# Retention attention followed by a gated feed-forward block on one core: products of 64x64 on quarters of TensorE for pairs 2 to 11

## The chip, the cores and the metric

The kernel runs on one core of a Trainium2 chip. The metric is the device time of one execution in microseconds (us). TensorE (PE in the profile, with its weight loads as PEld) multiplies matrices into PSUM; VectorE (DVE), ScalarE (ACT) and GpSimd (POOL) do the elementwise work; SyncE (SP) issues transfers. Each engine takes its instructions in the order in which the kernel lists them.

## The reference, cut to what matters

Two stages follow each other, on 4 batch entries, 8 heads, 768 tokens and head size 64; the feed-forward block has model width 512 and inner width 1536.

```python
gamma = 1.0 - 2.0 ** (-5.0 - arange(H))
for t in range(S):
    state = gamma * state + einsum('bhd,bhe->bhde', k[:, :, t], v[:, :, t])
    y[:, :, t] = D ** -0.5 * einsum('bhd,bhde->bhe', q[:, :, t], state)
x = y.transpose(0, 2, 1, 3).reshape(B * S, H * D)
out = (sigmoid(x @ w_gate) * (x @ w_val)) @ w_out
```

## The kernel before, in words

**Tiles and pairs.** The 768 tokens are 6 token tiles of 128. A tile holds 4 batch entries; the kernel takes them two at a time, so there are 12 pairs P (tile P // 2, entries 2(P % 2) and the next, called c = 0 and 1). The recurrence is done in chunks: within a tile by scores, across tiles by a running state.

**The steps of a pair.** Each step is a short function that emits instructions; a two-letter name and a number call it from a list.

- `lk`, `lq`, `lv`: GpSimd loads k, q, v of a pair (L64), tokens on partitions. A tile of 1024 columns holds 16 heads of 64.
- `xk`, `xq` (pairs 4 to 11): SyncE issues one transposing transfer of the whole tile (L197) into `qkT`, so that head dimensions lie on partitions. Two heads share a block of 128 partitions: head 2p in the lower half, 2p+1 in the upper. For pairs 2 and 3 TensorE transposes (`tp`, L178) and ScalarE copies (`te`, L188).
- `sc`: scores of one entry, eight products with 64 rows of contraction and 128 columns of output (L216), two running side by side on the upper and lower half of the array, into two PSUM banks. `sd` is both entries.
- `mk`: VectorE multiplies four heads of scores with the decay mask (L221); four of these for a pair. The number is 4P + 2c + i.
- `in`: the inter products, query with the state of earlier tiles (L233). The state of two heads lies block-diagonally in `zbd`, with zeros beside it, so each product contracts over 128 rows and gives 64 columns; two run side by side on the left and right half. `id` is both entries.
- `ia`: the intra products, masked scores with v (L239), added on the same bank. `il` is both entries. `yo`: VectorE scales the result into `xT`, the input of the feed-forward block (L254). The number of `in`, `ia`, `yo` and `sc` is 2P + c.
- `kt`, `sm`, `zs`, `zo`: keys are scaled (L206, L209), k times v is formed (L261), added to the state on VectorE (L270), and copied to `zbd` by ScalarE in two halves (L274, two steps).
- `ho`: a tiny copy on GpSimd (L556) that reads the last transposed element of a pair, so that later loads are issued only after that.

**The feed-forward block** is done for one token tile at a time (512 rows). From tile 3 on, and for the down projection from tile 0 on, it uses products of halves with sums and differences prepared beforehand, so it has many small steps: `gm`, `vm`, `ag`, `av`, `bg`, `bv`, `vp` (up products, L284 whole or L288 split), `sg`, `as`, `bs` (sigmoids on ScalarE), `mu`, `am`, `bm` (gating on VectorE), `vc`, `va`, `vf` (copy, add and finish), `dm`, `dp`, `dc`, `da`, `ds` (down products, copy, add and store), and the sums `hs`, `hh` (VectorE, L460), `xs` (VectorE), `aw`, `dw`, `wp` (GpSimd, L339 and L443).

**Whole and split products.** A step in small letters emits its products in column halves: 128 rows by 64 columns, two side by side (L288). In capitals it emits 128 by 128 (L284). So the array is used in three shapes: 128x128, 128 rows x 64 columns, and 64 rows x 128 columns (only the scores).

**What sets the order.** Nothing is scheduled automatically. `ORDER` is one string for each token tile; its steps are emitted in that order, `+` and `-` shift a step to a later or an earlier tile. The place of a step fixes the place of its instructions in the queue of every engine that it uses. PSUM gives seven banks to everything but the state products, which have an eighth to themselves.

Of the kernel before, what the change touches and what calls it, by code (L numbers as in the profile page):

```python
# [17 lines left out]
def kernel(  # L18
# [40 lines left out]

    def load(P, *what):  # L60
        for n in what:
            held, x = {"k": (kn, k), "q": (qn, q), "v": (vn, v)}[n]
            held[P] = ld.tile([C, 2 * H, D], BF16, tag=n, name=n + "n", bufs=4)
            nc.gpsimd.dma_start(out=held[P], in_=src(x, P))  # L64

    def load_one(P, c, *what):
        for n in what:
            held, x = {"k": (kn, k), "q": (qn, q), "v": (vn, v)}[n]
            if P not in held:
                held[P] = ld.tile([C, 2 * H, D], BF16, tag=n, name=n + "n", bufs=4)  # L70
            t, j = divmod(P, 2)
            nc.gpsimd.dma_start(out=heads(held[P], c),
                                in_=x[2 * j + c, :, t * C:(t + 1) * C, :].rearrange("h s d -> s h d"))
# [56 lines left out]
    zbd = [const.tile([128, 2, NP, C], BF16, name=f"zbd{i}") for i in range(2)]  # L130
    for z in zbd:
        nc.vector.memset(z, 0.0)
# [33 lines left out]
    def new_qkT(P):  # L166
        qkT[P] = ld.tile([128, 2, 2, NP, C], BF16, tag="qkT", name="qkT", bufs=4)
# [3 lines left out]
    def transpose(P, i, cs):  # L171
        tp = bank([128, 2 * NP, C], BF16).rearrange("d (c p) s -> d c p s", c=2)
        x = (kn, qn)[i][P].rearrange("s g d -> s (g d)")
        for c in cs:
            for p in range(NP):
                for lo, n in ((0, C),) if whole[0] else ((0, D), (D, D)):
                    at_p = (c * NP + p) * C + lo
                    nc.tensor.transpose(tp[lo:lo + n, c, p, :], x[:, at_p:at_p + n], ident)  # L178
        turned[P, i] = tp

    def turned_out(P, i, cs, *evict):
# [5 lines left out]
        for c, e in zip(cs, evict):  # L187
            (nc.scalar.copy if e == "a" else nc.vector.tensor_copy)(qkT[P][:, i, c], tp[:, c])  # L188
# [5 lines left out]
    def xbar(P, i):  # L194
        if P not in qkT:
            new_qkT(P)
        nc.sync.dma_start_transpose(out=qkT[P][:, i].rearrange("d c p s -> d (c p) s"),  # L197
                                    in_=(kn, qn)[i][P].rearrange("s g d -> s (g d)"))
# [12 lines left out]
    def scores(P, c):  # L211
        sc[P, c] = (bank([128, NP, C]), bank([128, NP, C]))
        for p in range(NP):
            for i in range(2):
                half = slice(i * D, (i + 1) * D)
                nc.tensor.matmul(sc[P, c][i][:, p, :], qkT[P][half, 0, c, p, :], qkT[P][half, 1, c, p, :],  # L216
                                 start=True, stop=True)

    def mask(P, c, i):
        st[P, c, i] = at.tile([128, NP, C], BF16, tag="st", name="st", bufs=8)  # L220
# [6 lines left out]
    def inter(P, c):  # L227
        y[P, c] = bank([128, NP, C])
        if P > 1:
            for p in range(NP):  # L230
                for i in range(2):
                    half = slice(i * D, (i + 1) * D)
                    nc.tensor.matmul(y[P, c][half, p, :], zbd[P % 2][:, c, p, half], qkT[P][:, 1, c, p, :],  # L233
                                     start=(p == 0), stop=False, skip_group_check=True)

    def intra(P, c):
        for p in range(NP):
            for i in range(2):
                nc.tensor.matmul(y[P, c][i * D:(i + 1) * D, p, :], heads(vn[P], c)[:, 2 * p + i, :],  # L239
                                 st[P, c, i][:, p, :], start=(P < 2 and p == 0), stop=True, skip_group_check=True)  # L240
# [15 lines left out]
    def state(P):  # L256
        zz[P] = pz.tile([128, 2, NP, D], F32, tag="z", name="z")
        for c in range(2):
            for p in range(NP):
                for i in range(2):  # L260
                    nc.tensor.matmul(zz[P][i * D:(i + 1) * D, c, p, :], heads(kt[P], c)[:, 2 * p + i, :],  # L261
# [10 lines left out]
    def state_out(P, i):  # L272
        half = slice(i * D, (i + 1) * D)
        nc.scalar.copy(zbd[P % 2][half, :, :, half], za[P % 2][half])  # L274
# [78 lines left out]
    def late_weight_sums(g, i):  # L353
        if g not in gws:
            tag = "qqqqkkk"[g]
            room = ld.tile([C, 2 * H, D], BF16, tag=tag, name=tag + "n", bufs=4)
# [198 lines left out]
    def hold(P):  # L555
        nc.gpsimd.tensor_copy(kept[:, :2], qkT[P][:, :, 1, NP - 1, C - 1])  # L556
# [5 lines left out]
    def y_step(P, c, eng="a"):  # L562
        inter(P, c)
# [49 lines left out]
    for s in range(4):  # L613
# [52 lines left out]
        "in": lambda t, n: inter(n // 2, n % 2),  # L666
        "sd": lambda t, P: [scores(P, c) for c in range(2)],
        "id": lambda t, P: [inter(P, c) for c in range(2)],
# [6 lines left out]
        "zo": lambda t, n: state_out(n // 2, n % 2),  # L675
# [92 lines left out]
```

## Time and profile before

| what | value |
|---|---|
| median of 3 runs | 221.34 us (220.79 to 224.9) |
| the profiled execution's own time | 221.63 us |
| its span, first to last instruction | 219.9 us |
| first product starts, last product ends | 2.0 us, 216.4 us |
| PE busy from 18 to 43 us of the span | 24.78 of 25 us |
| PE busy from 43 to 66 us | 23.00 of 23 us |
| PE busy from 66 to 220 us | 150.43 of 154 us |
| DVE, ACT, POOL busy | 158.4, 116.3, 131.1 us |
| granted TensorE clock | 1.000 |

The span is taken by the hardware profiler; 1.7 us of the execution's own time lie around it. Groups of instructions are listed by source line, engine, operation and tiles; behind the bar stand the busy time of the group, the mean duration of one instruction, and the idle time of the engine before them. Matmuls overlap, so the mean of one (some 220 ns for 128 columns) is its latency, not what it adds: that is seen in the timeline, where the start of the next group follows. The chain of work that ended last goes back from the end of the program, at each step to what released it.

### The profile page before, as it was taken

To read this page: it belongs to the slowest core of one execution; us is meant where nothing else is said; L and a number is where in the kernel's file an instruction comes from. 1 tells how busy PE (TensorE), PEld (TensorE's weight loads), DVE (VectorE), ACT (ScalarE), POOL (GpSimd) and SP (SyncE) were. 2 spreads that over 40 slices of the span, in tenths; PEclk is the share of its full clock that TensorE was granted. 3 is DMA by queue.
4 is the path that set the end of the run, shared out by engine and by line. 5 is a ranking of instruction groups with operands and counts; after the bars stand their busy time and mean duration, and the time that the engine had idled before them with its cause. 6 is when DMAs were issued, how large, how long until landed. Compare 5 with 4: busy or idle time off the path is not lost.

```text
span 219.9 us, 6868 instructions
## 1 busy us (share of the span) xinstructions
PE 210.8 (96%) x2906; PEld 163.2 (74%) x2906; DVE 158.4 (72%) x330; ACT 116.3 (53%) x254; POOL 131.1 (60%) x149
## 2 busy tenths in 40 slices
PE   6778999999999999999999999999999999999993
PEld 6565455799888767777778877789877866887782
DVE  6574865988649799766898677699775776555771
ACT  7474366437856165743729554525356626354431
POOL 8978785779997993597037733660281660166700
PEclk9999999999999999999999999999999999999999
DMA  9999999999995999599993999800520000022005
GB/s 127 136 171 195 193 174 160 194 190 157 144 113 93 157 156 167 131 173 166 123 185 46 162 211 149 92 0 3 146 98 0 3 1 3 0 95 97 3 1 192
DMA packets 103999, 25.35 MB, mean 115 GB/s; under 512 B 93984, under 2 KB 101152, under 8 KB 103968
## 3 DMA queue, kind: packets, MB, share of 16 engines
q0 software_dynamic: 81248, 13.90, 84.1%
q1 hardware_dynamic: 22576, 10.88, 27.8%
q8 instruction: 22, 0.36, 0.7%
q10 hardware_dynamic: 144, 0.13, 0.2%
q14 instruction: 9, 0.07, 0.1%
HBM read 28.31 MB, written 6.29 MB: 157 GB/s over the span
## 4 chain that ended last, share of the span: by engine, by line
PE 94%; DVE 3%; ACT 1%; issue 1%; DVEq 0%
PE ff L288 53%; PE ff L284 28%; PE ff L216 3%; PE ff L178 2%; PE ff L239 2%; PE ff L531 2%; PE ff L233 2%; PE z L261 1%; DVE st L221 1%; DVE qkT L188 1%; ACT xT L252 0%; DVE qn L572 0%; DVE xT L252 0%; DVE lgp L117 0%; ACT ob L504 0%
## 5 line engine op out<-in xcount | busy, mean ns | idle before, releaser
L308 ACT ACTIVATE gs<-ff 128x512 f32<-128x512 f32 (+1 forms) x61 | 35.7, 591 | 35.1 <-PE ff L288 23.0
L288 PE MATMUL ff<-xT,wg 128*64 128x512 bf16 (+1 forms) x408 | 48.4, 363 | 0.0
L405 POOL TENSOR_TENSOR hT<-gs,scr 128x512 bf16<-128x512 f32 x17 | 21.9, 1291 | 40.0 <-DVE scr L399 35.9
L288 PE MATMUL ff<-xT,wv 128*64 128x256 bf16 (+1 forms) x352 | 35.7, 324 | 0.0
L288 PEld LDWEIGHTS <-wg 128*64 128x64 bf16 x408 | 23.0, 110 | 10.3 <-issue 0.2
L399 DVE TENSOR_TENSOR scr<-scr,ff 128x256 f32<-128x256 f32 x51 | 20.4, 415 | 13.1 <-PE ff L284 6.0
L288 PEld LDWEIGHTS <-wv 128*64 128x64 bf16 x388 | 21.9, 110 | 8.6
L221 DVE TENSOR_TENSOR st<-ff,maskd 128x512 bf16<-128x512 f32 x40 | 25.7, 683 | 3.5 <-PE ff L216 3.4
L284 PE MATMUL ff<-xT,wg 128*128 128x256 bf16 (+1 forms) x136 | 25.2, 323 | 1.5 <-ACT xT L252 0.9
L311 DVE TENSOR_TENSOR hT<-gs,ff 128x512 bf16<-128x512 f32 (+1 forms) x27 | 17.7, 664 | 7.9 <-PE ff L284 3.0
L288 PEld LDWEIGHTS <-hT 128*64 128x64 bf16 x372 | 20.5, 110 | 3.2
L514 DVE TENSOR_TENSOR ob<-p,ff 128x256 f32<-128x256 f32 x33 | 13.6, 416 | 10.0 <-ACT p L506 4.5
L284 PEld LDWEIGHTS <-wg 128*128 128x128 bf16 x136 | 13.1, 98 | 8.3 <-issue 0.9
L408 POOL TENSOR_TENSOR hT<-gs,scr 128x256 bf16<-128x256 f32 x17 | 12.6, 747 | 6.6 <-DVE scr L399 6.1
L209 ACT ACTIVATE kt<-kn,tabk 128x128 bf16<-128x128 bf16 x48 | 16.4, 393 | 0.0
L254 DVE TENSOR_TENSOR xT<-ff,taby 128x512 bf16<-128x512 f32 x20 | 13.5, 685 | 3.4 <-PE ff L239 3.4
L288 PE MATMUL ff<-wo,hT 128*64 128x256 bf16 (+1 forms) x204 | 15.7, 292 | 0.0
L284 PE MATMUL ff<-xT,wv 128*128 128x256 bf16 (+1 forms) x96 | 15.5, 290 | 0.0
L64 POOL DMA_DIRECT2D vn<-in_v_dram x12 | 14.0, 1170 | 2.3 <-DMA wo<-in_moe_w_out_dram 0.8
L64 POOL DMA_DIRECT2D kn<-in_k_dram x11 | 12.9, 1175 | 3.3 <-DMA vn<-in_v_dram 1.7
L288 PEld LDWEIGHTS <-hs 128*64 128x64 bf16 x252 | 13.7, 110 | 0.4
L274 ACT CAST zbd<-za 64x512 bf16<-64x512 f32 x20 | 12.2, 613 | 3.3 <-DVE za L268 3.1
(108 smaller groups left out, 411.9 us busy)
## 6 DMA issues: line engine op xcount, KB each, us to landing
out_dram<-ob SPq DMA_DIRECT2D x22, 256.0 KB, 2.6
vn<-in_v_dram POOLq DMA_DIRECT2D x12, 256.0 KB, 11.1
kn<-in_k_dram POOLq DMA_DIRECT2D x11, 256.0 KB, 10.3
qn<-in_q_dram POOLq DMA_DIRECT2D x11, 256.0 KB, 11.8
wo<-in_moe_w_out_dram POOLq DMA_DIRECT2D x4, 384.0 KB, 13.0
wg<-in_moe_w_gate_dram POOLq DMA_DIRECT2D x5, 256.0 KB, 9.2
wv<-in_moe_w_val_dram POOLq DMA_DIRECT2D x5, 256.0 KB, 9.3
out_dram<-ob SPq DMA_DIRECT2D x3, 128.0 KB, 2.2
```

The source lines that it names most:

```text
L64: nc.gpsimd.dma_start(out=held[P], in_=src(x, P))
L209: nc.scalar.activation(to[:, :, h, :], x[:, :, h, :], AX.Copy, scale=tabk[:, P // 2, h:h + 1])
L221: nc.vector.tensor_tensor(st[P, c, i], sc[P, c][i], (mask0 if P < 2 else maskd[P // 2])[:, i], op=ALU.mult)
L254: nc.vector.tensor_tensor(o, y[P, c], taby[t], op=ALU.mult)
L284: nc.tensor.matmul(o, left, right, skip_group_check=True, **kw)
L288: nc.tensor.matmul(o[half], left[:, half], right, skip_group_check=True, **kw)
L308: nc.scalar.activation(gated[t, n1][:, lo:hi], us[t, n1, 0][:, lo:hi], AX.Sigmoid)
L311: nc.vector.tensor_tensor(hidden(t)[:, n1, lo:hi], gated[t, n1][:, lo:hi], us[t, n1, 1][:, lo:hi], op=ALU.mult)
L399: nc.vector.tensor_tensor(o, o, (b if n == 5 else ac)[:, :256], op=ALU.add)
L405: nc.gpsimd.tensor_tensor(h[:, 2 * g], s, vals[t, g][:, 0:2].rearrange("p two n -> p (two n)"), op=ALU.mult)
L408: nc.gpsimd.tensor_tensor(h[:, 2 * g + 1, 256:], s[:, 256:], vals[t, g][:, 2], op=ALU.mult)
L514: nc.vector.tensor_tensor(o, x, z, op=ALU.add)
```

## The change

It does five things.

1. For pairs 2 to 11 a score product is cut into two halves of its output rows, 64 rows by 64 columns each (four quarters of the array are used in turn): 16 products in place of 8 for each entry, the same columns streamed.
2. The inter products contract over the 64 rows of their own head only, on one quarter of the array: 16 products of 64 by 64 for a pair, as many as before. Both entries are emitted as one step `id`. The heads of the second entry (c = 1) lie exchanged: what was in the lower half of the partitions lies in the upper, so its products read the other quarters. `zb` holds the state without zeros.
3. The state goes to `zb` in one ScalarE copy of 128 partitions (`zo`, one step) in place of two of 64. The two memsets of `zbd` at the start are gone.
4. To get the exchanged layout, the transposing transfer is issued as two: the first entry's four blocks, and five blocks that begin one head earlier for the second. k and q tiles are 64 columns wider, and GpSimd clears these columns with a memset before it issues the load (pairs 4 to 11). TensorE's transposes for pairs 2 and 3 place each head by itself; their number stays. The tiles `st` have 7 buffers in place of 8.
5. `ORDER` is new from the first tile's last third on, for all engines.

The intra step of a pair names the last four inter products as what it depends on; in the built program no product waits for a semaphore on that account.

```diff
+    def natural(n, P):
+        if n == "v":
+            return ld.tile([C, 2 * H, D], BF16, tag=n, name=n + "n", bufs=4)
+        wide[n, P] = ld.tile([C, 2 * H + 1, D], BF16, tag=n, name=n + "n", bufs=4)
+        if P > 3:
+            nc.gpsimd.memset(wide[n, P][:, 2 * H], 0.0)
+        return wide[n, P][:, :2 * H]
...
-    zbd = [const.tile([128, 2, NP, C], BF16, name=f"zbd{i}") for i in range(2)]
-    for z in zbd:
-        nc.vector.memset(z, 0.0)
+    zb = [const.tile([128, 2, NP, D], BF16, name=f"zb{i}") for i in range(2)]
...
+    def place(P, c, h):
+        return h % 2 ^ (c if P > 1 else 0), c * NP + (h + (c if P > 3 else 0)) // 2
+
+    def of(P, i, c, h):
+        r, b = place(P, c, h)
+        return qkT[P][r * D:(r + 1) * D, i, b, :]
...
-        nc.sync.dma_start_transpose(out=qkT[P][:, i].rearrange("d c p s -> d (c p) s"),
-                                    in_=(kn, qn)[i][P].rearrange("s g d -> s (g d)"))
+        x = wide["kq"[i], P].rearrange("s g d -> s (g d)")
+        nc.sync.dma_start_transpose(out=qkT[P][:, i, :NP], in_=x[:, :H * D])
+        nc.sync.dma_start_transpose(out=qkT[P][:, i, NP:], in_=x[:, (H - 1) * D:])
...
-                half = slice(i * D, (i + 1) * D)
-                nc.tensor.matmul(sc[P, c][i][:, p, :], qkT[P][half, 0, c, p, :], qkT[P][half, 1, c, p, :],
-                                 start=True, stop=True)
+                h = 2 * p + i
+                for u in range(1 if P < 2 else 2):
+                    own = slice(0, C) if P < 2 else slice(u * D, (u + 1) * D)
+                    nc.tensor.matmul(sc[P, c][i][own, p, :], of(P, 0, c, h)[:, own], of(P, 1, c, h),
+                                     start=True, stop=True)
...
-        st[P, c, i] = at.tile([128, NP, C], BF16, tag="st", name="st", bufs=8)
+        st[P, c, i] = at.tile([128, NP, C], BF16, tag="st", name="st", bufs=7)
...
-                    nc.tensor.matmul(y[P, c][half, p, :], zbd[P % 2][:, c, p, half], qkT[P][:, 1, c, p, :],
-                                     start=(p == 0), stop=False, skip_group_check=True)
+                    r, _ = place(P, c, 2 * p + i)
+                    m = nc.tensor.matmul(y[P, c][i * D:(i + 1) * D, p, :], zb[P % 2][r * D:(r + 1) * D, c, p, :],
+                                         of(P, 1, c, 2 * p + i), start=(p == 0), stop=False, skip_group_check=True)
...
-    def state_out(P, i):
-        half = slice(i * D, (i + 1) * D)
-        nc.scalar.copy(zbd[P % 2][half, :, :, half], za[P % 2][half])
+    def state_out(P):
+        nc.scalar.copy(zb[P % 2], za[P % 2])
...
     ORDER = [
...
-        "gm9 vm9 sg9 mu9 tp4 te4 tp5 te5 gm10 vm10 sg10 mu10 sc4 sc5 sm2 mk8 mk9 mk10 mk11 gm11 vm11 sg11 in4+  "
-        "in5+ ia4+ ia5+ yo4+ yo5+ mu11 zs2+ kt24+ tp6+ te6+ tp7+ te7+",
+        "sg9 mu9 tp4 te4 tp5 te5 gm10 vm10 sc4 mk8 sc5 gm11 sg10 mk10 mk9 mk11 tp6+ id2+ ia4+ sg11 ia5+ yo4+  "
+        "tp7+ vm11 yo5+ te6+",
...
-        "wc4 ho5 mk17 dm6- am10 lk6 kt37 mk21 wc5 mk22 hh9- in11 hh11- kt39 mk20 lq6 aw16+ mk23 kt40 dc05- yo9  "
-        "in8 ia8 kt44 ia11 in10 dm7- yo8 ia10 lv6 yo11 lk7 lq7 da05- dp03- dp06- dc06- do3- dt3- lv7 bm10 yo10  "
-        "dp02 hh10- kt43 kt42 kt53+ tt10 sm4",
+        "sc10 aw12+ mk22 kt37 hh11- da05- lq6 dp03- wc5 kt38 id4 id5 kt40 kt45 mk21 kt46 ia8 kt41 mk23 ia9 kt39  "
+        "dp06- ia11 mk20 lv6 aw2+ dm6- kt47 lk7 ia10 kt34 bv10 dm7- dt1- kt44 kt53+ yo11 sm4 hs4 hh6- yo8 yo10  "
+        "lq7 aw14+ wp11 dp01 hh10- aw8+ yo9 aw16+",
-        "gm3 vm1 gm1 gm2 da06-- ds06-- hs0- kt45- zs4- dp07-- hs1- aw12 xk6- aw8 sg1 vm0 vm5 aw1 sm5- da07--  "
+        "gm3 dc06-- lv7- do3-- vm1 hs0- bm10- kt42- gm2 sg2 aw1 da06-- hs8- dt3-- zs4- hs9- dp07-- ds06-- gm0  "
...
```

More of the change, by code (lines that the diff above doesn't have):

```diff
@@ L58, in src @@
         return x[2 * j:2 * j + 2, :, t * C:(t + 1) * C, :].rearrange("b h s d -> s (b h) d")
+    wide = {}
+    def natural(n, P):
[5 more added lines that the diff above has]
+        return wide[n, P][:, :2 * H]
     def load(P, *what):
@@ L62, in load @@
             held, x = {"k": (kn, k), "q": (qn, q), "v": (vn, v)}[n]
-            held[P] = ld.tile([C, 2 * H, D], BF16, tag=n, name=n + "n", bufs=4)
+            held[P] = natural(n, P)
             nc.gpsimd.dma_start(out=held[P], in_=src(x, P))
@@ L69, in load_one @@
             if P not in held:
-                held[P] = ld.tile([C, 2 * H, D], BF16, tag=n, name=n + "n", bufs=4)
+                held[P] = natural(n, P)
             t, j = divmod(P, 2)
@@ L166, in new_qkT @@
     def new_qkT(P):
-        qkT[P] = ld.tile([128, 2, 2, NP, C], BF16, tag="qkT", name="qkT", bufs=4)
+        qkT[P] = ld.tile([128, 2, 2 * NP + 1, C], BF16, tag="qkT", name="qkT", bufs=4)
+    def place(P, c, h):
[3 more added lines that the diff above has]
+        return qkT[P][r * D:(r + 1) * D, i, b, :]
     whole, turned = [True], {}
@@ L175, in transpose @@
             for p in range(NP):
-                for lo, n in ((0, C),) if whole[0] else ((0, D), (D, D)):
-                    at_p = (c * NP + p) * C + lo
-                    nc.tensor.transpose(tp[lo:lo + n, c, p, :], x[:, at_p:at_p + n], ident)
+                if P < 2:
+                    nc.tensor.transpose(tp[:, c, p, :], x[:, (c * NP + p) * C:(c * NP + p + 1) * C], ident)
+                    continue
+                for r in range(2):
+                    g = 2 * (c * NP + p) + (r ^ c)
+                    nc.tensor.transpose(tp[r * D:(r + 1) * D, c, p, :], x[:, g * D:(g + 1) * D], ident)
         turned[P, i] = tp
@@ L187, in turned_out @@
         for c, e in zip(cs, evict):
-            (nc.scalar.copy if e == "a" else nc.vector.tensor_copy)(qkT[P][:, i, c], tp[:, c])
+            (nc.scalar.copy if e == "a" else nc.vector.tensor_copy)(
+                qkT[P][:, i, :2 * NP].rearrange("d (c p) s -> d c p s", c=2)[:, c], tp[:, c])
     def transposes(P, i, cs, *evict):
@@ L225, in masks, with inter @@
             mask(P, c, i)
[L227 to L230, printed above, removed]
-                for i in range(2):
-                    half = slice(i * D, (i + 1) * D)
-                    nc.tensor.matmul(y[P, c][half, p, :], zbd[P % 2][:, c, p, half], qkT[P][:, 1, c, p, :],
-                                     start=(p == 0), stop=False, skip_group_check=True)
+    begun = {}
+    def inter(P):
+        y[P, 0], y[P, 1] = bank([128, NP, C]), bank([128, NP, C])
+        begun[P] = []
+        for p in range(NP):
+            for c in range(2):
+                for i in range(2):
+                    r, _ = place(P, c, 2 * p + i)
+                    m = nc.tensor.matmul(y[P, c][i * D:(i + 1) * D, p, :], zb[P % 2][r * D:(r + 1) * D, c, p, :],
+                                         of(P, 1, c, 2 * p + i), start=(p == 0), stop=False, skip_group_check=True)
+                    if p == NP - 1:
+                        begun[P].append(m.ins)
     def intra(P, c):
@@ L238, in intra @@
             for i in range(2):
-                nc.tensor.matmul(y[P, c][i * D:(i + 1) * D, p, :], heads(vn[P], c)[:, 2 * p + i, :],
-                                 st[P, c, i][:, p, :], start=(P < 2 and p == 0), stop=True, skip_group_check=True)
+                m = nc.tensor.matmul(y[P, c][i * D:(i + 1) * D, p, :], heads(vn[P], c)[:, 2 * p + i, :],
+                                     st[P, c, i][:, p, :], start=(P < 2 and p == 0), stop=True,
+                                     skip_group_check=True)
+                if begun.get(P):
+                    for b in begun.pop(P):
+                        tc.add_manual_dep(m.ins, b.name, mybir.DependencyInfo(
+                            mybir.DependencyClass.Sync, mybir.DependencyReason.DATA), reason="other rows")
     def y_out(P, c, eng="a"):
@@ L260, in state @@
                 for i in range(2):
-                    nc.tensor.matmul(zz[P][i * D:(i + 1) * D, c, p, :], heads(kt[P], c)[:, 2 * p + i, :],
+                    r = i ^ c
+                    nc.tensor.matmul(zz[P][r * D:(r + 1) * D, c, p, :], heads(kt[P], c)[:, 2 * p + i, :],
                                      heads(vn[P], c)[:, 2 * p + i, :], start=True, stop=True, skip_group_check=True)
@@ L270, in state_sum @@
             nc.vector.tensor_tensor(za[j], za[j], zz[P], op=ALU.add)
-    def state_out(P, i):
-        half = slice(i * D, (i + 1) * D)
-        nc.scalar.copy(zbd[P % 2][half, :, :, half], za[P % 2][half])
+    def state_out(P):
+        nc.scalar.copy(zb[P % 2], za[P % 2])
     hT = {}
@@ L355, in late_weight_sums @@
             tag = "qqqqkkk"[g]
-            room = ld.tile([C, 2 * H, D], BF16, tag=tag, name=tag + "n", bufs=4)
+            room = ld.tile([C, 2 * H + 1, D], BF16, tag=tag, name=tag + "n", bufs=4)[:, :2 * H]
             gws[g] = room.rearrange("p (i kk a) d -> p i kk (a d)", i=4, kk=KT // 2)
@@ L555, in hold @@
     def hold(P):
-        nc.gpsimd.tensor_copy(kept[:, :2], qkT[P][:, :, 1, NP - 1, C - 1])
+        nc.gpsimd.tensor_copy(kept[:, :2], qkT[P][:, :, 2 * NP, C - 1])
     def hold_for_sums(t):
@@ L562, in y_step @@
     def y_step(P, c, eng="a"):
-        inter(P, c)
+        y[P, c] = bank([128, NP, C])
         intra(P, c)
@@ L665 @@
         "sc": lambda t, n: scores(n // 2, n % 2),
-        "in": lambda t, n: inter(n // 2, n % 2),
         "sd": lambda t, P: [scores(P, c) for c in range(2)],
-        "id": lambda t, P: [inter(P, c) for c in range(2)],
+        "id": lambda t, P: inter(P),
         "il": lambda t, P: [intra(P, c) for c in range(2)],
@@ L674 @@
         "zs": lambda t, P: state_sum(P),
-        "zo": lambda t, n: state_out(n // 2, n % 2),
+        "zo": lambda t, P: state_out(P),
     }
```

92 rows, old and new, of the table ORDER are left out of this document.

## The prediction

> **What bounds the kernel now.** I read the page's busy times first, then the windows by stage, then the chain in order of time, then the groups with their shapes kept apart, and at last the timelines of SP, DVE and POOL around the places that the new order touches.
>
> ```profile
> span 219.9 us, 6868 instructions
> ...
> PE 210.8 (96%) x2906; PEld 163.2 (74%) x2906; DVE 158.4 (72%) x330; ACT 116.3 (53%) x254; POOL 131.1 (60%) x149
> ...
> PE 94%; DVE 3%; ACT 1%; issue 1%; DVEq 0%
> ```
>
> The first two lines are the page's head and part 1, the third opens part 4. TensorE is busy for 96% and is 94% of the chain. The table above says where the rest is: 0.2 us idle between 18 and 43 us, none from 43 us to the last product at 216.4 us. So until something else runs late, the time is the length of TensorE's stream, and relief for another engine gives nothing.
>
> ```profile
> 46.52 0.55 PE ff L216 x16
> ...
> 50.94 0.45 PE ff L233 x16
> 51.38 0.45 PE ff L239 x16
> ```
>
> These are pieces of the chain: start, length, what. Sixteen products of 128 columns take 0.45 us (inter, intra), because two run side by side: eight rounds of 56 ns. In the trace the second of a round starts 3 to 4 ns after the first, the next round 52 or 53 ns after that. The sixteen score products are eight such rounds too, and take 0.55. The 0.10 above is the change from 64x128 back to 128x64. Single starts show both ways: 205 ns from the last 256-column round to the first score product where the next round would start after 106, and 145 ns from the last score product where 52 is usual. I take 96 ns for a change of shape, the mean of the 99 and the 93.
>
> ```profile
> L216 PE MATMUL ff<-qkT 64*128 64x128 bf16 x192 | 8.7, 225 | 0.6 <-DVE qkT L188 0.5
> ...
> L233 PE MATMUL ff<-qkT,zbd 128*64 128x128 bf16 x160 | 7.1, 219 | 0.0
> ...
> L274 ACT CAST zbd<-za 64x512 bf16<-64x512 f32 x20 | 12.2, 613 | 3.3 <-DVE za L268 3.1
> ```
>
> The groups by shape give the counts and the state copy's price.
>
> **The change part by part.** The profiled execution took 221.63 us, 0.29 above the median of 221.34. I sum against it and take the sum to the median at the end.
>
> *Inter products.* Ten pairs, 0.45 us each now. Afterwards the 16 products are four rounds of four. No row shows four at once. A round is at least the 56 ns of a round of two, and at most that plus two more starts of 3.5 ns, 63. I take 60, since starts cost 3 to 4 ns wherever they are seen: 0.24 a pair, 0.21 saved, **-2.1** in all (-2.0 to -2.25).
>
> *Scores.* Twenty entries, now four rounds of 56 = 0.224. Afterwards 16 products in four rounds of four, 0.24 by the same choice: **+0.3** (0 to +0.56).
>
> *Changes of shape.* Counted in the two built programs, TensorE's stream changes shape 38 times before and 55 after, because `id` steps now stand alone between 128x64 work. 17 at 96 ns: **+1.6**. Forty of the 55 are between 64x64 and 128x64, where only the rows change, and no row shows that kind. The lower bound is nothing for these 40: 15 x 0.096 against 38 x 0.096, -2.2. I take 96 ns, because both kinds that are seen, one that changes rows and columns and one that changes columns alone (128x128 to 128x64, 202 where 109 is usual), cost the same. The page TensorEngine Tiling (Array Packing) of the Trainium skill, Key Properties, says that changing the tiling mode, not just the tile, drains TensorE; the 0.10 of L216 agrees, and by that rule the +1.6 stands, which speaks against this change.
>
> *State copy and memsets.* ScalarE loses ten copies of 0.61 us, DVE two memsets of 0.49 at 3 to 4 us. ScalarE is off the path at 53%, and DVE's next work there waits for a load that lands at 3.9 us: **0**.
>
> *Transposing transfers.* Sixteen issues become 32, with nine blocks moved where there were eight, all on SP's queue; stores behind them (`ds`, `dt`) wait for two issues.
>
> ```profile
> 51.59 1.35 SPq L197 DMA_TRANSPOSE qkT<-kn  x1
> 53.43 4.18 SPq L197 DMA_TRANSPOSE qkT<-qn  x1
> 57.66 2.41 SPq L197 DMA_TRANSPOSE qkT<-kn  x1
> 61.51 1.79 SPq L197 DMA_TRANSPOSE qkT<-qn  x1
> ```
>
> This is SP's timeline (start, length of the issue). Pair 4's two land by 63.86 us and its scores start at 65.39; pair 5's by 67.01, used at 68.89. So 1.5 and 1.9 us to spare. Four later ones in a quiet stretch (issued from 82.13, landed by 90.07) need 2.0 us each. Lower bound: an eighth more, 0.25 each, hidden. Upper: each second issue costs another 1.3 us, so pair 4 is 2.6 late and pair 5 5.2, stalls of 1.1 and up to 3.3. I stay near the lower end, since the 4.18 is an issue held up by transfers still under way, so bytes rule there: **+0.3**. Later pairs have 3 us (pair 11) or over 5 to spare, and `xq11` no longer stands behind a store. The 16 memsets on POOL (98 ns for a tiny one, 186 for the tiny copy) add 1.6 to 3 us to an engine at 60%; what waits behind them are loads, which land in a row 1.85 us apart: 0.
>
> *The new order, masks of pair 2.* Four masks take 2.48 us in the chain at 38.99, 0.62 apart. From the start of `sc4` TensorE now has `sc4`, `sc5` (0.24 each), `gm11` 0.87, `tp6` 0.45, `id2` 0.24 and three changes of shape, 2.3 us, before `ia4`, and 2.55 before `ia5`. The masks are done 0.45 + 4 x 0.62 = 2.9 us after it. So 0.4 us of waiting in place of the 0.2 idle now: **+0.2**.
>
> *The new order before `gm3`.* `gm3` needs all four `yo8` to `yo11`. Ahead of the last, `yo9`, DVE's queue now has `hs4`, `hh6` and `hh10`; before, only `hh10`, behind the last `yo`. Their price depends on POOL, as DVE's and POOL's timelines show:
>
> ```profile
> 76.39 0.68 DVE L254 TENSOR_TENSOR xT<-ff,taby 128x512 bf16<-128x512 f32 x1
> 77.00 4.34 DVE L460 TENSOR_TENSOR hT<-hT 128x256 bf16<-128x256 bf16 x1
> ```
>
> ```profile
> 77.11 1.31 POOL L339 TENSOR_TENSOR ws<-ws,wv 128x256 bf16<-128x256 bf16 x2
> 78.37 0.67 POOL L339 TENSOR_TENSOR ws<-wv 128x256 bf16<-128x256 bf16 x1
> 78.99 1.03 POOL L157 TENSOR_TENSOR taby<-taby,tabz 128x512 f32<-128x512 f32 x1
> 79.99 1.16 POOL L443 TENSOR_TENSOR wt<-wo,scr 128x512 bf16<-128x512 bf16 x1
> ```
>
> An operation that takes 0.28 us elsewhere (L460 at 32.57) took 4.34 while POOL ran one elementwise instruction after another; the `yo` before it (L254, one operand in PSUM) did not suffer. In the new order POOL has `aw14`, `wp11`, `aw8`, `aw16` in a row there, 0.69 + 1.19 + 0.69 + 0.69 = 3.3 us. From `ia10` to `gm3` TensorE has `bv10`, `dm7`, `sm4`, `dp01`: 0.87 + 1.31 + 0.25 + 0.66 = 3.1. DVE needs three `yo` and `hh10`, 3 x 0.62 + 0.3, and the tail of `hs4`: about 2.5. So 0.6 us to spare if POOL is elsewhere, and a stall of up to 2.7 if not. Lower bound 0, upper 2.7; POOL reaches `aw14` about when DVE reaches `hh10`, more likely just later, so I take **+0.3**. The page SBUF — State Buffer of the Trainium skill, Who interferes with whom, says that a DVE instruction with two SBUF inputs and a GpSimd instruction that reads SBUF shut each other out for whole instructions; the 4.34 agrees, and by that rule alone the stall would be a matter of who starts first.
>
> Sum: -2.1 + 0.3 + 1.6 + 0.3 + 0.2 + 0.3 = +0.6. Against 221.63 that is 222.2; against the median 221.9.
>
> **The rivals.**
>
> *A, the sum above:* TensorE stays the bound and what the inter products save goes to the changes of shape. **221.9**, by itself 220.4 to 223.4.
>
> *B, a change of rows alone is free.* -2.2 in place of +1.6, so 3.8 less: **218.1**. For it: no row shows this kind. Against: the two kinds seen cost the same.
>
> *C, the other side: the quarters run two at a time, not four.* Then inter keeps eight rounds (+2.1 against my sum), and the scores get eight rounds where they had four (20 x (0.448 - 0.24) = +4.2): **228.2**. For it: no row shows 64x64. Against: two halves run side by side in either direction, 3 to 4 ns apart. It decides from rounds of some 100 ns on: 120 rounds (40 of inter, 80 of scores) at 40 ns more are 4.8.
>
> *D, DVE shut out before `gm3`, or at another such place* (`hh4` ahead of `yo6` and `yo7`, `BG2` right behind them): 2.7 to 4.3 us more, **225** in the middle. For it: the 4.34, and DVE at 72% in front of a TensorE with no slack. Against: of L460's 72 rows six took over 0.9 us, and only that one over 1.3.
>
> *E, the transfers of pairs 4 and 5 come late:* stalls up to 3.3, **224**. Against: bytes rule there.
>
> **How the numbers follow.** A 0.62, B 0.08, C 0.10, D 0.13, E 0.07. The time is A's. The range is 219.4 to 226.0. It leaves out C (0.10), the end of D (0.03) and the larger half of B (0.05); B at half the price lies at 220.0 and within. 2% of the median is 4.4 us, about what a measurement of this kernel can tell from no change: faster means under 216.9, which only B with a further 1.2 us reaches, 0.03. Slower means over 225.8: C with 0.10, and 0.04 from D and E where two stalls add up. The rest, 0.83, is within 2%.
>
> **What would show it.** Right: four starts 3 to 4 ns apart at the inter products' line, rounds of 56 to 63 ns, 16 of them in 0.24 us; some 96 ns at each entry and exit of 64x64; TensorE without idle time after 43 us but for a few tenths near 41 and before the third tile. Wrong: inter products still 0.45 a pair (C); no extra time at the edges (B); a single idle gap of 2 us or more before L316 or L320, with a long DVE L492 ahead of it (D); PE waiting for the transposes at 66 or 70 us (E). A gap at a place that I have not worked through would make the prediction wrong most simply.

## The result and the profile after

| | kernel before | changed kernel |
|---|---|---|
| median of 21 runs each | 221.75 us | 222.91 us |
| lowest | 220.79 us | 222.17 us |
| profiled execution, its own time | 221.63 us | 222.17 us |
| first up product starts, last product ends | 15.93, 216.43 us | 15.07, 217.02 us |
| stretch between the two | 200.50 us | 201.95 us |

The ratio is 1.0053, 95% interval 1.0027 to 1.0078: the change costs 0.6 to 1.7 us. Two slow runs of the changed kernel, 226.33 and 226.93 us, are left out of it. The forecast was +0.6, 221.9, in a range of 219.4 to 226.0. The start phase up to the first up product differs by 0.86 us between the two profiles, so the table compares the stretch behind it: +1.45 us.

The head, part 1 and the first line of part 4 of the page after:

```profile
span 220.5 us, 7213 instructions
...
PE 209.4 (95%) x3060; PEld 160.1 (73%) x3066; DVE 160.7 (73%) x328; ACT 108.6 (49%) x244; POOL 133.7 (61%) x165
...
PE 88%; DVE 4%; DMA 3%; POOL 2%; ACT 1%; issue 1%; POOLq 0%; DVEq 0%
```

TensorE is still the bound. Its share of the chain is 88% where it was 94%, but that is no measure of the loss: DMA's 3% and POOL's 2% lie before 11.7 us, where the chain of this execution goes back through a load, as that of the kernel before does not. Behind the start phase there is one new place where the chain leaves TensorE, VectorE's work from 73.25 to 79.20 us. The groups with their shapes, for the lines that replace L216, L233 and L274:

```profile
L238 PE MATMUL ff<-qkT 64*64 64x128 bf16 x320 | 7.3, 220 | 0.0
...
L258 PE MATMUL ff<-qkT,zb 64*64 64x128 bf16 x160 | 4.0, 221 | 0.0
...
L306 ACT CAST zb<-za 128x512 bf16<-128x512 f32 x10 | 6.1, 612 | 3.2 <-DVE za L301 3.2
```

The ten wide state copies take 612 ns each, as the twenty narrow ones did (613). The chain from the scores of pair 4 to the third tile (start, length, what):

```profile
64.78 0.57 PE ff L238 x32
...
71.20 0.57 PE ff L258 x32
71.77 0.57 PE ff L266 x16
...
73.25 0.69 DVE xT L286
73.95 0.53 DVE hs L492
74.48 0.68 DVE hT L492
75.15 1.20 DVE xT L286 x2
76.35 2.24 DVE hT L492
78.59 0.61 DVE xT L286
79.20 0.04 issue
79.25 10.58 PE ff L320 x120
```

The first two lines hold what was meant: the 32 score products of one pair in 0.57 (before, 16 in 0.55), and the 32 inter products of two pairs in 0.57 with one change of shape in it (before, the 16 of one pair in 0.45 without one). The rest is a chain on VectorE. TensorE's timeline shows 1.44 us of idle time ahead of `gm3`, its only idle time over 0.2 us behind the start phase, and VectorE's and GpSimd's show what ran then:

```profile
79.25 1.05 PE L320 MATMUL ff<-xT,wg 128*64 128x512 bf16 x8 [1.44 <-DVE xT L286]
```

```profile
76.28 2.32 DVE L492 TENSOR_TENSOR hT<-hT 128x256 bf16<-128x256 bf16 x1
```

```profile
76.62 0.69 POOL L371 TENSOR_TENSOR ws<-wv 128x256 bf16<-128x256 bf16 x1
77.26 1.17 POOL L475 TENSOR_TENSOR wt<-wo,scr 128x512 bf16<-128x512 bf16 x1
```

The sum `hh10` (the second `hT L492` of the chain) took 2.24 us there, 2.32 with the part that overlaps the instruction before it. Beside it GpSimd ran `aw14` and `wp11`.

So the 1.45 us of the stretch are, in size, this one wait. TensorE's stream otherwise nets about nothing. Whether that is cause or coincidence is what the first experiments ask.

### The profile page after: what moved, and what is told of

Read it like the earlier page. It is cut to its first block, busy times and chain, and to the rows that moved or that the text cites. A ratio compares the mean times of both kernels' runs of the same rounds, so it can differ in the third digit from the quotient of the medians.

```text
span 220.5 us, 7213 instructions
## 1 busy us (share of the span) xinstructions
PE 209.4 (95%) x3060; PEld 160.1 (73%) x3066; DVE 160.7 (73%) x328; ACT 108.6 (49%) x244; POOL 133.7 (61%) x165
## 4 chain that ended last, share of the span: by engine, by line
PE 88%; DVE 4%; DMA 3%; POOL 2%; ACT 1%; issue 1%; POOLq 0%; DVEq 0%
PE ff L320 51%; PE ff L316 28%; DMA qn<-in_q_dram 3%; PE ff L238 3%; PE ff L266 2%; DVE hT L492 1%; PE ff L258 1%; PE z L294 1%; DVE xT L286 1%; DVE st L243 1%; PE ff L196 1%; POOL kn L74 1%; ACT xT L284 0%; POOL kn L82 0%; POOL qn L82 0%
## 5 line engine op out<-in xcount | busy, mean ns | idle before, releaser
L320 PE MATMUL ff<-xT,wg 128*64 128x512 bf16 (+1 forms) x408 | 47.8, 363 | 1.4 <-DVE xT L286 1.4
L243 DVE TENSOR_TENSOR st<-ff,maskd 128x512 bf16<-128x512 f32 x40 | 26.2, 683 | 8.6 <-PE ff L238 6.6
L546 DVE TENSOR_TENSOR ob<-p,ff 128x256 f32<-128x256 f32 x33 | 13.5, 417 | 9.2 <-ACT p L538 3.5
L316 PEld LDWEIGHTS <-wv 128*128 128x128 bf16 x112 | 10.8, 98 | 4.5 <-issue 0.4
L424 ACT COPY scr<-ff 128x512 f32<-128x512 f32 x17 | 9.9, 587 | 8.5 <-PE ff L320 3.3
```

The lines of the kernel that those rows point to most:

```text
L243: nc.vector.tensor_tensor(st[P, c, i], sc[P, c][i], (mask0 if P < 2 else maskd[P // 2])[:, i], op=ALU.mult)
L316: nc.tensor.matmul(o, left, right, skip_group_check=True, **kw)
L320: nc.tensor.matmul(o[half], left[:, half], right, skip_group_check=True, **kw)
L424: nc.scalar.copy(vals[t, g][:, 0:3:2], ac.rearrange("p (two n) -> p two n", two=2))
L546: nc.vector.tensor_tensor(o, x, z, op=ALU.add)
```

## The experiments

Theory W: the loss is the wait before `gm3`, made by VectorE's sums (two bf16 operands in SBUF) being shut out by GpSimd's. Theory S: the loss is in the stream, in score products and changes of shape. Theory T: it is the doubled transfers, or the new order as a whole. "Stretch" is always from the first up product's start to the last product's end in the profiled execution.

**1. The sums behind `yo9`.**

```diff
-kt53+ yo11 sm4 hs4 hh6- yo8 yo10 lq7 aw14+ wp11 dp01 hh10- aw8+ yo9 aw16+
+kt53+ yo11 sm4 yo8 yo10 lq7 aw14+ wp11 dp01 aw8+ yo9 hs4 hh6- hh10- aw16+
```

> The changed kernel with hs4, hh6 and hh10 behind yo9 in the order; nothing else moves. Theory W (the 1.2 us lost are the one wait before gm3, where hh10 took 2.24 us ahead of yo9, and TensorE's stream nets about nothing): the gap before the third tile's first product goes from 1.44 us to under 0.3, the time falls by 1.2 to 1.4 to about 221.6, ratio to the kernel before 0.999 to 1.001. Rival S (the loss is in the stream itself, that is in the score products and the changes of shape): the gap closes but as much is lost elsewhere, or the gap was cover for something else that is late: still 222.9, ratio 1.005.

Measured: 220.8 us, ratio 0.9972 (0.9947 to 0.9996). The stretch is 200.53 us. TensorE's wait before `gm3` is gone; a wait of 0.09 us is left further on, behind the moved sums. Its chain there:

```profile
74.75 1.29 DVE xT L286 x2
76.04 0.79 DVE hs L492
76.82 1.84 DVE hT L492 x2
78.67 0.81 DVE hs L492
79.48 0.60 DVE hT L360
80.08 0.34 DVE ob L546
80.42 0.04 issue
80.46 3.54 PE ff L320 x38
```

The sums are slow here too (1.84 us for two, where one takes 0.28 elsewhere), but now `gm3` and what follows run meanwhile. Moving three of VectorE's instructions took away 1.42 us of stretch: W holds, S would have left them. It is also faster than the kernel before, if by little.

**2. GpSimd's sums later, VectorE's order untouched.**

```diff
-lq7 aw14+ wp11 dp01 hh10- aw8+ yo9 aw16+
+lq7 wp11 dp01 hh10- yo9
...
-xq6- aw9 tt9-
+xq6- tt9-
...
-sg5 hi0-
+sg5 hi0- aw14 aw8 aw9 aw16
```

> The changed kernel with GpSimd's sums aw14, aw8, aw16 (and aw9, which needs aw8) put behind hi0, some 8 us later, where GpSimd is idle; VectorE's order is untouched, and wp11 stays. Theory L (VectorE's bf16 sum with two SBUF operands is shut out by GpSimd's instructions): hh10 takes 0.3 us, or up to 1.5 where it meets wp11, in place of 2.24; gap before gm3 under 0.7, time 221.6 to 222.2, ratio 0.999 to 1.003. Rival Q (VectorE is simply late with three more operations in its queue, GpSimd has no part): hh10 keeps its 2.2 us and the gap its 1.4: 222.9, ratio 1.005.

Measured: 222.8 us, ratio 1.0053 (1.0024 to 1.0082). That misses the 221.6 to 222.2 of theory L; it is the time of rival Q. The profiled execution had a granted clock of 0.5 and 0.8 in two slices between 11 and 22 us, so its stretch is no measure either. What can be read are durations, in VectorE's and GpSimd's timelines:

```profile
78.02 1.19 DVE L492 TENSOR_TENSOR hT<-hT 128x256 bf16<-128x256 bf16 x1
```

```profile
77.87 1.18 POOL L475 TENSOR_TENSOR wt<-wo,scr 128x512 bf16<-128x512 bf16 x1
```

`hh10` fell from 2.24 to 1.12 in the chain, and the idle gap from 1.44 to 0.81, a little over the 0.7 expected. What is left of `hh10`'s delay coincides with `wp11`, the one GpSimd sum that still stands there. The sum before it, `hh6`, became longer, 1.25 us (75.64 to 76.90) where the changed kernel has 0.75; at that time GpSimd issued a load (75.45 to 76.64) and cleared a strip.

**3. `wp11` later as well**, on top of experiment 2. From `lk7` to `gm3` GpSimd then only issues loads and clears two strips.

```diff
-gm2 sg2 aw1 da06--
+gm2 sg2 aw1 wp11- da06--
```

(and `wp11` taken out ahead of `dp01`)

> As e2_pool_later, with wp11 put behind lv7 and aw1 as well, so that before gm3 GpSimd has only loads to issue and two clearings of 64 columns. In e2 hh10 took 1.19 us, just as long as wp11 beside it, and the gap before gm3 fell from 1.44 to 0.81. If only GpSimd's elementwise instructions shut VectorE out: hh10 0.3 us, gap under 0.1, time 220.8 to 221.5, ratio 0.997 to 1.000. If issuing a load does the same (in e3 a triple of such sums took 2.15 us in place of 1.09 when it started 0.08 us after a load's issue, and TensorE waited 0.60): hh10 some 1.2 us, gap about 0.8, 222.2 or more, ratio 1.002 to 1.005.

Measured: 220.82 us, ratio 0.9957 (0.9933 to 0.9981). The profiled execution took 223.88 us, with a granted clock of 0.69 from 11 to 22 us and 1.00 from 76 to 82, so the durations below can be read and its stretch can't. VectorE's timeline:

```profile
78.87 0.47 DVE L492 TENSOR_TENSOR hT<-hT 128x256 bf16<-128x256 bf16 x1
79.27 0.68 DVE L286 TENSOR_TENSOR xT<-ff,taby 128x512 bf16<-128x512 f32 x1
```

`hh10` took 0.47 us although a load was being issued beside it (78.06 to 79.21), and `gm3` does not wait. (This execution has another wait, 0.70 us at 50.26, which experiment 8 explains.) VectorE's order is that of the changed kernel, so rival Q falls: the price of `hh10` is that of GpSimd's sums. The instruction ends tell the same. In the changed kernel, in e1 and in e2 `hh10` ends 0.16 us after `wp11` ends (78.59 and 78.43, 78.67 and 78.51, 79.21 and 79.05), whenever it began.

**4. One part alone: score products cut, in the kernel before.**

```diff
-                nc.tensor.matmul(sc[P, c][i][:, p, :], qkT[P][half, 0, c, p, :], ...
+                for u in range(1 if P < 2 else 2):
+                    own = slice(0, C) if P < 2 else slice(u * D, (u + 1) * D)
+                    nc.tensor.matmul(sc[P, c][i][own, p, :], qkT[P][half, 0, c, p, own], ...
```

> The kernel before with one part of the change alone: each score product of pairs 2 to 11 cut into two halves of 64 output rows. Order, layout, inter products and the number of shape changes (38) stay, but the changes at the scores become those of rows alone (64x64 to 128x64). By the sum (change of rows alone 96 ns like the others, four quarters in a round of 60 ns): +0.3, 222.05, ratio 1.0014. By rival B (a change of rows alone is free): about 34 changes cheaper, -3 us, ratio 0.987. By rival C (two quarters at a time): +4.2 us, ratio 1.019.

Measured: 222.26 us, ratio 1.0025 (1.0000 to 1.0050). Rivals B (0.987) and C (1.019) are out. Part of the +0.5 is again a meeting: three sums at 91.56 us took 2.15 us where the kernel before has 1.09, because the third met GpSimd's decay table (92.62 to 93.28), and TensorE waited 0.60. At each of the 13 places where pairs 2 to 11 have scores, the cut products end 18 ns later than the whole ones, 0.24 us in all.

**5. One part alone: two transfers each, in the kernel before.**

```diff
-        nc.sync.dma_start_transpose(out=qkT[P][:, i].rearrange("d c p s -> d (c p) s"), ...
+        for c in range(2):
+            nc.sync.dma_start_transpose(out=qkT[P][:, i, c], ...
```

> The kernel before with another part alone: each transposing transfer issued as two of four blocks. Theory W: nothing waits for them, as in the changed kernel, where the transposes of pairs 4 and 5 landed before they were used: ratio 1.000, no idle time of TensorE at 64 to 70 us. Rival E (each second issue costs SP another 1.3 us): pair 4 is 2.6 us late and pair 5 5.2, stalls of 1.1 to 3.3 us before their scores: ratio 1.005 to 1.015.

Measured: 222.72 us, ratio 1.0038 (1.0006 to 1.0071). Pairs 4 and 5 do not wait, so rival E is wrong in its place. But there is a wait of 1.02 us elsewhere, and its chain names it:

```profile
91.63 2.48 DMA qkT<-qn
...
94.23 0.05 POOL kept L557
...
94.89 0.64 POOL kn L64
...
97.24 0.67 POOL maskd L152
97.93 0.70 DVE st L222
98.62 0.04 issue
98.67 0.84 PE ff L289 x12
```

The last transpose of pair 7 lands at 94.1 us (90.07 in the kernel before). `ho7` holds GpSimd until then; two loads and the decay table of pair 6 stand behind it, then VectorE's mask, then TensorE. The changed kernel's transposes are as late (SyncE's timeline: eight issues where there were four),

```profile
81.43 1.24 SPq L217 DMA_TRANSPOSE qkT<-kn  x1
...
92.33 1.23 SPq L218 DMA_TRANSPOSE qkT<-qn  x1
```

and its `ho7` comes at 95.05, yet TensorE shows no gap there. Its masks of pair 6 start at 96.61, no later than the 96.48 of the kernel before; but its order has the decay table (`tt9`) ahead of `ho7`, and GpSimd's timeline shows it done long before:

```profile
84.05 0.81 POOL L160 TENSOR_SCALAR_AFFINE_SELECT maskd<-tabk 128x512 f32<-128x512 f32 x1
```

**6. The changed code in the order of the kernel before** (`id` at the first `in`, `zo` at the second; 58 changes of shape).

> The changed products, layout and transfers in the order of the kernel before: id stands where the first of the two in steps stood, one zo where the second stood; 58 changes of shape. By the sum: inter -2.1, scores +0.3, 20 changes +1.9, and the doubled transfers +1.0 as in e4 (there TensorE waited 1.02 us for pair 6's masks, behind GpSimd's hold, two loads and the decay table): 222.7, ratio 1.005. If the new order is to blame for the changed kernel's loss as a whole: 221.6 or less, ratio 1.000.

Measured: 224.11 us, ratio 1.0097 (1.0059 to 1.0135), so more than the sum gave. The new order is not to blame: with this code it is, if anything, worth about 1 us (1.0053 against 1.0097, with intervals that overlap). The profiled execution was the fastest run (222.64) and shows only part of the loss: waits of 0.1 to 0.4 us at 48, 99 and 167 us, the last two inside inter products. What the other runs lost beyond the sum's 222.7 stays open.

**7. Fewer changes of shape.** On top of experiment 1: `sc11 sc10 id4 id5` in a row, `sc13` beside `id6`.

> e1_sums_behind with six changes of shape fewer, 49: sc11, sc10, id4, id5 in a row with dp02 ahead and dp03 behind, and sc13 moved next to id6 and sc12. The same instructions otherwise. If each change costs some 96 ns: 0.6 us less than e1, 220.2, ratio 0.9945. If changes are free, or the masks and banks that the moved steps need come late: 220.8 or more, ratio 0.997 or above, in the second case with an idle gap of TensorE at 70 to 74 or 100 to 105 us.

Measured: 224.66 us, ratio 1.0126 (1.0086 to 1.0167). The second case. The chain:

```profile
69.71 0.36 PE ff L238 x14
...
70.70 0.71 DVE hs L492
71.41 0.33 DVE ob L546
71.74 0.61 DVE st L243
72.36 0.04 issue
72.40 0.41 PE ff L258 x14
```

The inter products wait for a mask, which they do not read: by the chain it has to free their bank. There are more waits, at 98.8 and 110.4 us, 3.1 us in all, for the 0.6 that fewer changes were to save.

**8. More changes of shape.** On top of experiment 1: the inter products of pairs 6 to 11 in two halves with one small step between, 12 changes more.

```diff
-vc35 vp26 id10 vc26
+vc35 ie10 vp26 if10 vc26
```

> e1_sums_behind with twelve changes of shape more, 67: the inter products of pairs 6 to 11 in two halves with one other small product step between them. The same instructions otherwise. At 96 ns a change: 1.15 us more than e1, 221.95, ratio 1.0024. If a change of rows alone is free and the 0.10 at such places is something else: 220.8, ratio 0.997.

Measured: 222.7 us, ratio 1.0046 (1.0022 to 1.0070), which is 1.6 us above e1's. The profiled execution took 224.19. Its stretch is 203.05, 2.52 above e1, but 0.78 of that is idle time of TensorE at 50 us, behind a meeting that e1 did not have. VectorE's and GpSimd's timelines of e7, and VectorE's of e1:

```profile
46.60 2.21 DVE L226 TENSOR_TENSOR kt<-kn,tabk 128x1024 bf16<-128x1024 bf16 x1
```

```profile
46.56 1.17 POOL L476 TENSOR_TENSOR scr<-wo 128x512 f32<-128x512 bf16 x1
47.67 1.63 POOL L160 TENSOR_SCALAR_AFFINE_SELECT maskd<-tabk 128x512 f32<-128x512 f32 x1
```

```profile
45.76 1.22 DVE L226 TENSOR_TENSOR kt<-kn,tabk 128x1024 bf16<-128x1024 bf16 x1
```

VectorE came 0.04 us after GpSimd and took 1.0 us longer than in e1; then GpSimd's table took 1.63 where 0.64 is usual. In e1 VectorE was first by 1.19 us and all but done when GpSimd began (46.95). In e7 VectorE reached this place 0.84 us later, as late as its first up product was (15.95 against 15.11).

**9 and 10. The same, with an order meant to avoid that meeting:** all sums apart (experiments 1 and 3 together) and `kt24` behind pair 3's masks; and on top of it the 12 changes.

> The changed kernel with every meeting of VectorE and GpSimd seen so far taken out: the sums hs4, hh6, hh10 behind yo9 (as e1), aw14, aw8, aw9, aw16 and wp11 later (as e5), and kt24 behind pair 3's four masks. The last is for a place that e5 and e7 showed: kt24 began 0.04 us after GpSimd's wp1, took 2.2 us in place of 1.2, and TensorE waited 0.7 to 0.8 at 50 us. If these waits are all that was lost and TensorE's stream nets 0.1 to 0.2 less than before: 220.4, ratio 0.995. If the sums are needed early by the down products: a gap at 80 to 95 us, ratio 0.998 or above.

> e9_no_meeting with the twelve more changes of shape of e7_more_changes, now without the meeting of kt24 and wp1. By the edges' starts (96 and 93 ns) 1.13 us more than e9; by e7 against e1 in the trace, the wait at 50 us taken off, some 1.7 us (0.14 each). If changes were free, the same as e9.

Measured: 222.67 us, ratio 1.0035 (1.0012 to 1.0059), and 224.43 us, ratio 1.0106 (1.0068 to 1.0145). As a cure e9 failed. `kt24` still met GpSimd (1.59 us in e9, 1.97 in e10), though TensorE's 0.78 is gone in e9; in e10 it waits 0.42 us at 52.34, behind the operations of VectorE that follow. The chain shows what e9 lost elsewhere:

```profile
76.49 0.83 DVE hs L492
77.33 2.86 DVE hT L492 x2
80.19 0.80 DVE hs L492
...
81.93 0.04 issue
81.97 7.99 PE ff L320 x96
```

The two edits of the sums helped alone; together they bring the sums and `wp11` side by side again, 2.86 us, and the down products wait 1.15 us for them. As a pair the two price a change: stretches 204.24 and 202.43, idle time 0.12 more in e10, so 1.69 us for 12, 0.14 each. From e7 and e1: (2.52 - 0.78) / 12 = 0.145. Counted only where the 12 lie, e7 and e1 give less: the same down products start 1.81 us later in e7 (82.27 and 80.46), the last product ends 3.36 later (219.00 and 215.64), so 1.55 for 12, 0.13 each.

**11. `kt24` alone behind the masks.**

> The changed kernel with kt24 behind pair 3's masks and nothing else. Its profiled execution was its fastest run (222.17, median 222.91) and had no wait at 50 us. If the meeting of kt24 and wp1 happens in many of its other runs and makes the 0.7 us between median and fastest: median 222.2 to 222.4, ratio 1.002. If it is rare there, or the spread is in the start phase: 222.9, ratio 1.005.

Measured: 223.06 us, ratio 1.0071 (1.0034 to 1.0108). No gain. `kt24` still met GpSimd here (1.68 us), but TensorE waits only 0.14 us for it, at 51.41, and 1.47 before `gm3` as in the changed kernel. So the wait at 50 us is not shown to be what sets the changed kernel's median above its fastest run, and what does stays open.

## Why the prediction was right, and its steps

The time lies in the range and in case A's own band, and the sign was right. So was the mechanism: what the inter products save goes to the changes of shape. Two terms were too small, the changes by 0.4 us and the wait before `gm3` by 1.1. The prediction's sign of being right, a few tenths of idle time before the third tile, did not come, and neither did that of rival D, a gap of 2 us or more: it was 1.44.

| step | forecast | measured |
|---|---|---|
| inter products | -2.1 | -2.3 |
| score products | +0.3 | +0.2 |
| 17 changes of shape | +1.6 | +2.0 |
| state copy, memsets | 0 | 0 |
| doubled transfers | +0.3 | 0 in this order (e4: 0.1 to 1.6 in the old one) |
| masks of pair 2 | +0.2 | +0.05 (idle 0.18 for 0.13) |
| sums before `gm3` | +0.3 | +1.44 |
| sum | +0.6 | +1.4 (stretch: +1.45) |

*Inter and score products.* Single starts in e1's trace show four products 3 to 4 ns apart, and undisturbed rounds 56 ns after each other. So four rounds are 0.224 us, the lower end of what was bounded; 0.45 - 0.224, ten times, is 2.3. Rival C is refuted. For the scores, 0.57 less 0.55, ten times; e3's 0.24 agrees.

*Changes of shape.* Right in kind, a quarter too small. The change of rows alone, which no row had shown, costs what the others do: 202 ns to the first inter round where 106 is usual, 146 ns back where 53 is usual. Rival B is refuted. Not foreseen: the second round after a change is late too, 80 ns in place of 56 on entry, 133 in place of 109 on return. That makes 0.12 each, 2.0 for 17. The runs with 12 more give 0.13 to 0.14 each; the difference is not resolved. The page TensorEngine Tiling (Array Packing) of the Trainium skill, Key Properties, says that a change of mode drains TensorE; the late rounds agree with it.

*Transfers.* The reason was wrong and the result nearly right, which was luck. "Bytes rule" failed: in the quiet stretch the eight issues need 13.5 us from first issue to last landing where four needed 7.9, so a second issue costs 1.4 us, the upper end of the bounds. Pairs 4 and 5 escaped because their transfers landed by 66.44 us all the same (before, 67.01). The later pairs had their room, but the step looked only at the scores; e4 shows that the way through `ho7`, two loads and the decay table has less room. That way had not been worked through; the new order escaped it because its table stood ahead of `ho7`.

*Sums before `gm3`.* The step that failed in size: "POOL reaches `aw14` about when DVE reaches `hh10`, more likely just later, so I take +0.3". `hh10` began at 76.28 and `aw14` at 76.62, later as was said, and it made no difference: `hh10` ended after `aw14` and `wp11` both. From the end of `ia10` (74.56) to that of `yo9` (79.19) VectorE needed 4.6 us where the working had 2.5, and `hh10` is 2.0 of the difference. The bounds (0 to 2.7) held it, and it is rival D at half its price. Experiments 1 and 3 show it from both sides: with VectorE's sums moved or GpSimd's moved, the loss is gone. The page SBUF — State Buffer of the Trainium skill, Who interferes with whom, says that such instructions exclude each other whole. In e7 the two durations agree with it. `hh10` does not fit as simply: it began 0.34 us before `aw14` and still ended behind `wp11`.

So what the inter products won was paid back by the changes of shape and the scores, and the wait came on top.

What stays open: how e5 at 220.82 and e1 at 220.8 come out under the kernel before by 0.3 to 0.4% when e1's stretch is 200.53 against 200.50. The start phases of single profiles differ by up to 1 us, more than that.

## What to carry to other kernels

Count the changes of array shape before cutting products smaller: here ten pairs won 0.23 us each, and a step of its own between other shapes gave back 0.24. Where TensorE has no slack, move VectorE's operations with two SBUF operands behind the one that TensorE waits for, and look at what GpSimd does at that time. One such meeting cost VectorE 1.0 us in e7, 2.0 in the changed kernel and 4.1 in the kernel before (4.34 where 0.28 is usual). Moving one meeting can make another (e9), and a later place in the order need not avoid it (`kt24` in e9, e10 and e11).

## What the runs showed that was not expected

- VectorE's wait is not one instruction: `hh10` lost two of GpSimd's in a row (0.69 and 1.17 us) though it had begun before the first.
- Issuing a load on GpSimd (1.15 to 1.19 us) held such a sum in some places and not in others. `hh10` took 0.47 us beside one in e5, and `kt24` in e1 its usual 1.22. But `hh6`, which takes 0.28 by itself, took 0.75 in the changed kernel and in e5, where nothing but a load was being issued beside it, and 1.25 in e2. That the load did it is not shown.
- In e7 two starts 0.04 us apart cost both engines 1.0 us; e1, whose order is the same up to pair 6, had no meeting there. An edit 50 us away and a start phase that differs by 0.84 us went with that, so sub-microsecond edits here can't be judged by one profile.
